# A normalised, gated FFN on one Trainium2 core: the second pair's down projection with tokens moving, and x turned through memory

## The chip, the cores and the metric

The kernel runs on one core of one Trainium2 chip. The metric is device time in microseconds of one execution. The kernel before has a median of 581.3 us over three runs (579.65 to 582.16). The profile is of one execution of the program.

The engines are named as in the profile: PE is TensorE (its weight loads are PEld), DVE is VectorE, ACT is ScalarE, POOL is GpSimd, SP is the queue of the sync engine, from which all transfers are issued here.

## The reference, cut to what matters

There are 2048 tokens of 512 channels. A layer normalisation, scaled and shifted by vectors from a condition, feeds a long convolution; its gated result is added to x. Then comes the part that this change touches:

```
h = layernorm(x) * (1 + cb) + sb          # per token, over 512 channels
g = silu(h @ w_gate)                      # 512 -> 1792
u = h @ w_up                              # 512 -> 1792
x = x + gb * ((g * u) @ w_down)           # 1792 -> 512
```

All of it is float32. The kernel splits each operand of these products into a high and a low part and multiplies in three passes (low x high, high x low, high x high).

## The kernel before

**Tokens and blocks.** x lies in four tiles `xt[0]` to `xt[3]`, of 128 tokens on the partitions by 4 rows of 512 channels each: four blocks of 512 tokens. Blocks 0 and 1 are the first pair, 2 and 3 the second.

**The FFN.** The 1792 hidden channels are cut into `NF` = 14 slices f of 128, two of which are a group g. The loop over n runs through the 14 slices for the first pair (q = 0, n = 2 to 13, the first two slices being done before it) and then again for the second (q = 1, n = 14 to 27). In this text a step is one n. A step makes gate and up for both blocks of the pair by seven products of half matrices instead of eight (Strassen-Winograd), each of six matmuls: two channel blocks by three passes, 128 x 128 stationary weights and 512 moving tokens. The products accumulate in PSUM tiles a, b, c (and d).

**Down.** Between the products stand groups of the down projection of slices that are finished. In the first pair and in the last group of the second, `down` uses 128 tokens of the activations as stationary operand and 512 output channels of w_down as moving one: six matmuls, and DVE adds the result to `xt` (`x<-x,dn`). In the other six groups of the second pair, `down_seven` applies the seven-product scheme over 2 slices, 2 blocks and 2 halves of 256 output channels: its stationary operand is 128 tokens of the activations, its moving one 256 columns of prepared weights (`wdb`, `wdt`). For each of two token pairs `i0` and each of seven products n it issues six matmuls, two token rows by three passes, into the two halves of one PSUM bank (da, db, dc), and DVE adds the bank to `xt[2 + t]`. Steps 16 to 27 each hold seven such groups, since a group's down follows two steps behind.

**The second norm of blocks 2 and 3.** While the first pair runs, the operands of the second are made. DVE takes mean and variance (`norm_stats`, steps 4 and 6), POOL turns them into scale and bias `rs`, and `norm2b` normalises two of the four rows of a block into a buffer `nn` of one copy, one row on ACT and one on DVE, twice per block. DVE turns 32 x 32 pieces in place (`half_t`). `half_put` writes the buffer to memory in four transfers; `half_get` reads it back in eight with channels on the partitions, into `hraw`. `half_s` applies the condition's scale and shift on ACT. Then `hraw` is split into the operands `B11`, `T1` and so on, from step 9 on.

**What sets the order.** Every engine works through its instructions in program order. The table `AT` and the calls of `also` hang functions on places (n, k): step n, behind the product numbered k. In a step the products run in the order 1, 5, 7, 2, 3, 6, 4 of these numbers (`PLACE`), so that (9, 7) is the third place of step 9 and (9, 4) its last. All transfers go through SP in program order: the weights of later steps (`ws`), the stores of prepared weights (`dw`, `ds`), w_down (`wds`), and the writes and reads of the norm. Weights are prepared on ACT, POOL and DVE a step ahead.

Of the kernel before, what the change touches and what calls it, by code (L numbers as in the profile page):

```python
# [27 lines left out]
G = 2  # L28
TB = 4
# [14 lines left out]
def adaln_h3_swiglu(ctx, tc, q, k0, v0, kT, vT, ssm, dskip, wgu, wdn, wmod, e_fwd, e_inv, w_c, out):  # L44
    nc = tc.nc
    pe, dve, act, pool, sp = (InOrder(tc, e) for e in (nc.tensor, nc.vector, nc.scalar, nc.gpsimd, nc.sync))
    cp = ctx.enter_context(tc.tile_pool(name="cp", bufs=1))
# [3 lines left out]
    dp = ctx.enter_context(tc.tile_pool(name="dp", bufs=1, space=bass.MemoryType.DRAM))  # L51
# [46 lines left out]
    ffn = {}  # L98
# [267 lines left out]
    away = {}  # L366
# [166 lines left out]
    def stats(xs, name, done=False, rows_=range(TB)):  # L533

        if name not in mvs:
            mvs[name] = cp.tile([P, 2 * TB], F32, name="mv" + name)
        mv = mvs[name]
        for i in rows_:
            if not done:
                bn[name, i] = cp.tile([P, 1, 6], F32, tag="bn1", name=f"bn{name}{i}", bufs=4)  # L540
                dve.bn_stats(bn[name, i][:, 0, :], xs[:, i, :])
            dve.bn_aggr(mv[:, 2 * i : 2 * i + 2], bn[name, i])
        if TB - 1 not in rows_:
            return None
        rs = cp.tile([P, 2, TB], F32, name="rs" + name)
# [7 lines left out]
    xt, st1 = {}, {}  # L553

    def load_x(t):
        a = e8([P, 4, D], F32, f"x{t}")
# [99 lines left out]

    raw_h, nrm = [], {}

    def norm2a(t, done=False):
        return stats(xt[t], f"b{t}", done)  # L660

    def norm2b(t, rs, h, split=True):

        n = nrm[t, h] = ffn["s"].tile([P, 2, D], F32, tag="nn", name=f"n{t}_{h}", bufs=1)
        for k in range(2):
            i = 2 * h + k
            if split and k:
                dve.tensor_scalar(
                    n[:, k], xt[t][:, i, :], rs[:, 0, i : i + 1], rs[:, 1, i : i + 1], op0=ALU.mult, op1=ALU.add
                )  # L670
            else:
                act.activation(
                    n[:, k], xt[t][:, i, :], AF.Identity, scale=rs[:, 0, i : i + 1], bias=rs[:, 1, i : i + 1]
                )

    NT = {}

    def norm_t(t, b):
# [15 lines left out]
        else:  # L694
            dve.tensor_scalar(dst, pt, sc, bi, op0=ALU.mult, op1=ALU.add)

    def half_t(t, h, k):

        v = nrm[t, h][:, k].rearrange("p (c x) -> p c x", x=32)
        dve.transpose(v, v)  # L700

    def half_put(t, h):

        v = nrm[t, h].rearrange("p k (c x) -> p (k c) x", x=32)
        m = away["n", t, h] = dp.tile([32, 32, 4, 32], F32, tag=f"n{t}{h}", name=f"naway{t}{h}")
        for z in range(4):
            sp.dma_start(m[:, :, z, :], v[32 * z : 32 * z + 32])

    def half_get(t, h):

        m = away["n", t, h].rearrange("d (k b y) z x -> y k d b (z x)", k=2, y=4)
        for y in range(4):
            for k in range(2):
# [47 lines left out]
    stage, AOP, WD, WG = {}, {}, {}, {}  # L761
# [114 lines left out]
    PASSES = ((1, 0), (0, 1), (0, 0))  # L876
# [14 lines left out]
    def down(q, g, t, i):  # L891

        parts = 2 if (q, g, t, i) == (1, NG - 1, 0, 3) else 1
        for h in range(parts):
            d = slice(h * D // parts, (h + 1) * D // parts)
            o = one("dn")[:, 0 : D // parts]
            for fl in range(G):
                for n, (wa, xa) in enumerate(PASSES):
                    pe.matmul(
                        o, acts[q, g * G + fl, t][:, xa, i * P : (i + 1) * P], WD[g][:, wa, fl, d],  # L900
                        start=(fl == n == 0), stop=(fl == G - 1 and n == 2),
                    )
            xv = xt[2 * q + t][:, i, d]
            dve.tensor_tensor(xv, xv, o, op=ALU.add)
            if g == NG - 1:
                sp.dma_start(out[:, 4 * (2 * q + t) + i, d], xv)
        if i == 3:
            for fl in range(G):
                slots.append(acts.pop((q, g * G + fl, t)))
# [7 lines left out]
    def down_seven(g, i0, n, bank_):  # L917

        k, t, dh = SUM[n]
        a, b = HOP[g][PROD[n][0]], WT[g][PROD[n][1]]  # L920
        more = k in bank_
        if not more:
            bank_[k] = one("d" + k)
        o = bank_[k].rearrange("p (i d) -> p i d", i=2)
        for ii in range(2):
            for m, (wa, xa) in enumerate(PASSES):
                pe.matmul(
                    o[:, ii], a[:, xa, (i0 + ii) * P : (i0 + ii + 1) * P], b[:, wa],
                    start=(not more and ii == m == 0), stop=(m == 2), skip_group_check=True,
                )  # L930
        xv = xt[2 + t][:, i0 : i0 + 2, dh * (D // 2) : (dh + 1) * (D // 2)]
        dve.tensor_tensor(xv, xv, o, op=ALU.add)
        if i0:
            slots.append(HOP[g].pop(PROD[n][0]))

    def sevens(g):
        for i0 in (0, 2):
            bank_ = {}
            todo.extend(("7", g, i0, n, bank_) for n in SUM)

    def downs(n):
        for _ in range(min(n, len(todo))):
# [681 lines left out]
    def release(n):  # L1624
# [32 lines left out]
    def also(n, k, fn, *a):  # L1657
        AT2.setdefault((n, k), []).append(lambda: fn(*a))

    for n, (t, h) in zip((6, 8, 10, 11), ((2, 0), (2, 1), (3, 0), (3, 1))):  # L1660
        also(n - 1, 2, half_t, t, h, 0)
        also(n - 1, 6, half_t, t, h, 1)
        also(n, 1, half_put, t, h)
        also(n, 3, half_get, t, h)
        also(n + 1, 5, half_s, t, h)
    for n in range(G, 2 * NF):
        q, f = n // NF, n % NF

# [110 lines left out]
```

## Time and profile before

| what | value |
|---|---|
| median of three runs | 581.3 us |
| span of the profiled execution | 577.7 us (the page gives no other time of it) |
| PE busy | 571.7 us, 99% |
| DVE, ACT, POOL busy | 448.3, 306.4, 318.0 us |
| granted TensorE clock | 1.000 |
| DMA | 106.98 MB, 185 GB/s |
| matmuls of 512 columns, a step of the first pair | 66 in 14.95 us |
| matmuls of 512 and 256 columns, a step of the second pair | 42 and 42 in 14.67 us |

Starts of instructions are counted from the start of the span. The steps that matter here start at 221.72 (step 5), 236.68, 251.63, 266.60, 281.56 (step 9), 296.80, 312.30 and 327.26 us (step 12); the down groups of the second pair run from 389.8 to 563.5 us. A row of the timeline gives start, length, engine, line and operation with output and inputs by the program's names; in brackets, how long the engine had been idle and what released it. Since one helper records every operation, all carry line 40; groups are told apart by their tiles.

### The profile page before, as it was taken

Reading aid. Unit: us, or ns where it says so; the run is one execution under the profiler, and the core shown is the slowest. Engines: PE = TensorE matmul, PEld = TensorE weight load, DVE = VectorE, ACT = ScalarE, POOL = GpSimd, SP = SyncE. Lnnn points to the kernel's source line nnn. Section 1 sums busy time; section 2 is a strip of 40 time slices with the busy share of each in tenths; the row PEclk is TensorE's granted clock in tenths of the full one; section 3 lists DMA queues with packets and bytes.
Section 4 is the critical chain, followed back from the end, with each engine's and each line's share of the span. In section 5 each row is a group of like instructions: output and inputs, shape, how many; then the busy total and the mean of one; then the engine's idle time right before and its main releaser. Section 6 shows DMA issues by size and latency. Waiting matters only on the chain.

```text
span 577.7 us, 10729 instructions
## 1 busy us (share of the span) xinstructions
PE 571.7 (99%) x4262; PEld 462.5 (80%) x4262; DVE 448.3 (78%) x622; ACT 306.4 (53%) x471; POOL 318.0 (55%) x298
## 2 busy tenths in 40 slices
PE   9999999999999999999999999999999999999997
PEld 9985476546888888888887888888888888888886
DVE  4999999998998766666576579858686868686766
ACT  3999989951754544445454566343424343434330
POOL 1349897689737866757475676461606161515210
PEclk9999999999999999999999999999999999999999
DMA  8966998998215454284939970454343434343403
GB/s 315 411 256 261 379 251 227 235 235 205 69 37 200 148 216 165 40 281 145 283 140 257 250 319 1 149 190 171 117 160 124 160 123 161 127 162 127 163 1 145
DMA packets 54435, 106.98 MB, mean 185 GB/s; under 512 B 19441, under 2 KB 36209, under 8 KB 48370
## 3 DMA queue, kind: packets, MB, share of 16 engines
q1 hardware_dynamic: 54386, 106.31, 56.0%
q8 instruction: 33, 0.54, 0.4%
q14 instruction: 16, 0.13, 0.1%
HBM read 71.69 MB, written 34.60 MB: 184 GB/s over the span
## 4 chain that ended last, share of the span: by engine, by line
PE 86%; DVE 5%; DMA 4%; ACT 1%; SPq 1%; issue 1%; POOL 0%; ACTq 0%; POOLq 0%; DVEq 0%
PE a L40 22%; PE dn L40 14%; PE c L40 11%; PE b L40 6%; PE da L40 6%; PE s L40 4%; PE g L40 4%; PE dc L40 3%; PE iv L40 3%; PE pk L40 3%; DMA wm<-in_wmod 2%; PE kvt L40 2%; PE px L40 2%; DMA away<-X 1%; PE kt L40 1%; PE db L40 1%
## 5 line engine op out<-in xcount | busy, mean ns | idle before, releaser
L40 PE MATMUL a<-op,wsum 128*128 128x512 f32 x432 | 110.9, 392 | 0.3 <-ACT r L40 0.2
L40 PEld LDWEIGHTS a<-op,wsum 128*128 128x128 f32 x432 | 78.7, 188 | 15.7 <-ACT r L40 0.7
L40 PE MATMUL dn<-wd,acts 128*128 128x512 f32 x360 | 90.4, 389 | 0.0
L40 PEld LDWEIGHTS dn<-wd,acts 128*128 128x128 f32 x360 | 67.5, 188 | 14.0
L40 ACT COPY p<-a 128x512 f32<-128x512 f32 x50 | 29.3, 587 | 57.2 <-PE a L40 57.2
L40 POOL TENSOR_TENSOR wa<-ws,wa 128x512 fp32r<-128x512 f32 (+1 forms) x28 | 32.9, 1196 | 41.1 <-ACT wa L40 41.1
L40 DVE TENSOR_TENSOR x<-x,dn 128x512 f32<-128x512 f32 (+1 forms) x65 | 43.4, 672 | 12.8 <-PE dn L40 12.5
L40 POOL TENSOR_TENSOR tb<-wds 128x256 f32<-128x256 f32 x12 | 8.9, 740 | 64.1 <-DVE wds L40 64.1
L40 DVE TENSOR_TENSOR b<-r,c 128x512 f32<-128x512 f32 x24 | 16.7, 696 | 32.9 <-ACT sg L40 32.9
L40 ACT COPY r<-a 128x512 f32<-128x512 f32 x24 | 14.1, 586 | 50.7 <-PE a L40 50.7
L40 PE MATMUL c<-op,wa 128*128 128x512 f32 x156 | 40.0, 392 | 0.0
L40 PE MATMUL c<-op,wsum 128*128 128x512 f32 x156 | 39.6, 389 | 0.0
L40 DVE STREAM_TRANSPOSE X<-X 128x1024 f32<-128x1024 f32 x16 | 37.6, 2415 | 0.8 <-ACT X L40 0.8
L40 POOL TENSOR_TENSOR wsum<-sr,wsum 128x512 fp32r<-128x512 f32 x28 | 38.1, 1381 | 0.0
L40 PE MATMUL b<-op,wa 128*128 128x512 f32 x144 | 36.9, 391 | 0.0
L40 POOL TENSOR_TENSOR wd<-wds,wd 128x512 fp32r<-128x512 f32 x14 | 18.3, 1329 | 29.1 <-ACT wd L40 29.1
L40 PEld LDWEIGHTS c<-op,wsum 128*128 128x128 f32 x156 | 29.3, 188 | 6.1
L40 DVE TENSOR_TENSOR x<-x,da 128x512 f32<-128x512 f32 x48 | 32.7, 681 | 1.2 <-PE da L40 1.1
L40 PEld LDWEIGHTS c<-op,wa 128*128 128x128 f32 x156 | 28.5, 188 | 5.7 <-DVE b L40 0.4
L40 PEld LDWEIGHTS b<-op,wa 128*128 128x128 f32 x144 | 26.3, 188 | 4.9
L40 POOL TENSOR_TENSOR s<-s,bcs 128x512 f32<-128x512 f32 x22 | 28.0, 1287 | 0.9
L40 POOL TENSOR_TENSOR sr<-ws 128x256 f32<-128x256 f32 x28 | 24.8, 885 | 5.3 <-issue 4.4
(193 smaller groups left out, 1351.1 us busy)
## 6 DMA issues: line engine op xcount, KB each, us to landing
ds<-wsum SPq DMA_DIRECT2D x12, 1024.0 KB, 8.0
wsum<-ds SPq DMA_DIRECT2D x12, 1024.0 KB, 6.4
dw<-wa SPq DMA_DIRECT2D x12, 768.0 KB, 6.3
wa<-dw SPq DMA_DIRECT2D x12, 768.0 KB, 4.3
ws<-in_wgu SPq DMA_DIRECT2D x16, 512.0 KB, 5.4
wds<-in_wdn SPq DMA_DIRECT2D x14, 512.0 KB, 7.1
wm<-in_wmod SPq DMA_DIRECT2D x6, 1024.0 KB, 10.1
away<-X SPq DMA_DIRECT2D x3, 2048.0 KB, 11.8
```

The costliest lines, as they stand in the source:

```text
L40: return lambda *a, **k: self.tc.keep_in_program_order(f(*a, **k))
```

## The change

Two things change together, because the first needs the second.

**Down with 512 tokens moving.** In `down_seven` the operands change sides: 128 of the 256 columns of the prepared weights are now stationary, and all 512 tokens of a block move. A group is three matmuls of 512 columns instead of six of 256. The same is done in `down` for the last group of the second pair, where both forms move 512 columns. The result has output channels on the partitions and tokens in the rows, so x of blocks 2 and 3 has to lie that way too, and the output is turned back after the kernel.

**x turned, and normalised after turning.** x itself is now turned: DVE turns 32 x 32 pieces of each row out of `xt` into the buffer (`turn`), `put_rows` writes it to memory in four transfers, and `get_rows` reads it back in four, twice as large as before, over `xt` itself. The statistics are turned as well (`turn_rs`), written in four tiny transfers (`put_rs`) and read back spread over all 128 partitions into `bcs` (`get_rs`). The norm is then a product and a sum with those rows, on two channel blocks at a time (`rows_op`, 128 x 1024, on DVE or POOL), and `rows_s` applies scale and shift on ACT with 512 columns instead of 256.

```diff
-    def norm2b(t, rs, h, split=True):
...
+    def turn(t, i):
+
+        h, k = i // 2, i % 2
+        if k == 0:
+            nrm[t, h] = ffn["s"].tile([P, NB * 4, 2, 32], F32, tag="nn", name=f"n{t}_{h}", bufs=1)
+        dve.transpose(nrm[t, h][:, :, k], xt[t][:, i].rearrange("p (c x) -> p c x", x=32))
+
+    def put_rows(t, h):
+
+        m = away["x", t, h] = dp.tile([32, NB * 4, 2, 4, 32], F32, tag=f"x{t}{h}", name=f"xaway{t}{h}")
         for z in range(4):
-            sp.dma_start(m[:, :, z, :], v[32 * z : 32 * z + 32])
...
+            sp.dma_start(m[:, :, :, z, :], nrm[t, h][32 * z : 32 * z + 32])
+
+    def get_rows(t, h):
+
+        m = away["x", t, h].rearrange("d (b y) k z x -> y d b (k z x)", y=4)
         for y in range(4):
-            for k in range(2):
-                i = (2 * h + k) * P
-                sp.dma_start(raw_h[0][32 * y : 32 * y + 32, t % 2, :, i : i + P], m[y, k])
...
+            sp.dma_start(xt[t][32 * y : 32 * y + 32, :, 2 * h * P : 2 * h * P + 2 * P], m[y])
+
+    def turn_rs(t):
+        dve.transpose(flat[t], flat[t])
+
+    def put_rs(t):
+
+        m = away["r", t] = dp.tile([2 * TB, 4, 32], F32, tag=f"r{t}", name=f"raway{t}")
+        for z in range(4):
+            sp.dma_start(m[:, z], flat[t][32 * z : 32 * z + 2 * TB])
+
+    def get_rs(t):
+        m = away["r", t].rearrange("(k i) z x -> k (i z x)", k=2)
+        sp.dma_start(bcs[:, 0:2, :], m.partition_broadcast(P))
+
+    def rows_op(t, a, k, e):
+
+        d = raw_h[0][:, t % 2, 2 * a : 2 * a + 2]
+        r = bcs[:, k, None, :].to_broadcast([P, 2, D])
+        e.tensor_tensor(d, d if k else xt[t][:, 2 * a : 2 * a + 2], r, op=ALU.add if k else ALU.mult)
+
+    def rows_s(t, a):
+
+        for b in (2 * a, 2 * a + 1):
+            d = raw_h[0][:, t % 2, b]
             act.activation(d, d, AF.Identity, scale=modT[:, 1, b : b + 1], bias=modT[:, 0, b : b + 1])
...
-        o = bank_[k].rearrange("p (i d) -> p i d", i=2)
-        for ii in range(2):
-            for m, (wa, xa) in enumerate(PASSES):
-                pe.matmul(
-                    o[:, ii], a[:, xa, (i0 + ii) * P : (i0 + ii + 1) * P], b[:, wa],
-                    start=(not more and ii == m == 0), stop=(m == 2), skip_group_check=True,
-                )
-        xv = xt[2 + t][:, i0 : i0 + 2, dh * (D // 2) : (dh + 1) * (D // 2)]
+        o = bank_[k]
+        for m, (wa, xa) in enumerate(PASSES):
+            pe.matmul(
+                o, b[:, wa, i * P : (i + 1) * P], a[:, xa],
+                start=(not more and m == 0), stop=(m == 2), skip_group_check=True,
+            )
+        xv = xt[2 + t][:, 2 * dh + i]
         dve.tensor_tensor(xv, xv, o, op=ALU.add)
...
+    plan(
+        2,
+        (5, 1, turn, 0),
+        (5, 5, turn, 1),
+        (5, 7, turn_rs),
+        (5, 3, put_rows, 0),
+        (5, 6, put_rs),
+        (6, 1, turn, 2),
+        (6, 7, turn, 3),
+        (6, 7, get_rs),
+        (6, 3, put_rows, 1),
+        (6, 4, get_rows, 0),
+        (7, 7, get_rows, 1),
+        (7, 6, rows_op, 0, 0, dve),
+        (7, 4, rows_op, 1, 0, pool),
+        (8, 6, rows_op, 0, 1, pool),
+        (8, 6, rows_s, 0),
+        (8, 4, rows_op, 1, 1, pool),
+        (9, 1, rows_s, 1),
+    )
...
```

Block 3 has a like plan: turns at (6, 4), (7, 4), (8, 3) and (8, 4), writes at (8, 1) and (9, 1), reads at (9, 6) and (10, 1), its products at (10, 2) on DVE and (10, 6) on POOL, its sums at (11, 1) on POOL and (11, 7) on DVE, scale and shift at (11, 3) and (12, 5).

How the plan lies in the engines' queues is seen at three places. The first is PE in step 16, where the second pair's down groups begin (a, b, c are the gate and up products, da, db, dc the down groups). Before:

```order
L40 MATMUL da<-wdb,acts 128x256 x6
L40 MATMUL a<-op,wsum 128x512 x6
L40 MATMUL dc<-wdt,acts 128x256 x6
L40 MATMUL b<-op,wa 128x512 x6
L40 MATMUL da<-wdt,acts_3931 128x256 x6
```

The same place of PE in the kernel after:

```order
L40 MATMUL da<-acts,wdb 128x512 x3
L40 MATMUL a<-op,wsum 128x512 x6
L40 MATMUL dc<-acts,wdt 128x512 x3
L40 MATMUL b<-op,wa 128x512 x6
L40 MATMUL da<-acts_3923,wdt 128x512 x3
```

The order is the same; each down group has three matmuls of twice the length.

The second place is ACT from the end of step 8 into step 9 (p1 and p2 are the copies of PSUM tile a behind the first and third product, n3_0 a row of block 3 that is normalised). Before:

```order
L40 CAST acts_1949<-a_3025 128x512
L40 COPY p1_3163<-a_3156 128x512
L40 CAST acts_1949<-c_3041 128x512
L40 ACTIVATE hraw_1934<-hraw_1934,modT_89 128x256 x4
L40 COPY p2_3192<-a_3156 128x512
L40 ACTIVATE n3_0_3194<-x3_790,rsb3_2882 128x512
L40 CAST wa_3197<-ws_3078 128x512
```

The same place of ACT in the kernel after:

```order
L40 CAST acts_1949<-a_3037 128x512
L40 ACTIVATE hraw_1934<-hraw_1934,modT_89 128x512 x2
L40 COPY p1_3179<-a_3172 128x512
L40 ACTIVATE hraw_1934<-hraw_1934,modT_89 128x512 x2
L40 CAST acts_1949<-c_3053 128x512
L40 COPY p2_3211<-a_3172 128x512
L40 CAST wa_3213<-ws_3090 128x512
```

The scale and shift of block 2 moved ahead of the copy p1 in one half and ahead of the cast in the other, and the normalising pass behind p2 is gone.

The third place is POOL in the same steps (wa, wsum and sr are gate and up weights being prepared). In the kernel after, behind the weights of step 9 and ahead of those of step 10:

```order
L40 TENSOR_TENSOR wa<-ws,wa 128x512
L40 TENSOR_TENSOR wa<-ws,wa 128x256
L40 TENSOR_TENSOR wsum<-sr,wsum 128x512 x2
L40 TENSOR_TENSOR hraw<-hraw,bcs 128x1024 x2
L40 TENSOR_TENSOR sr<-ws 128x256
L40 TENSOR_TENSOR sr<-sr,ws 128x256
```

The row of hraw is new: the two sums of block 2, for which the activations of the second place wait. Before, sr followed wsum directly.

More of the change, by code (lines that the diff above doesn't have):

```diff
@@ L544, in stats @@
             return None
-        rs = cp.tile([P, 2, TB], F32, name="rs" + name)
+        if name[0] == "b":
+            flat[int(name[1])] = f = cp.tile([P, 32], F32, name="rs" + name)
+            dve.memset(f, 0.0)
+            rs = f[:, 0 : 2 * TB].rearrange("p (k i) -> p k i", k=2)
+        else:
+            rs = cp.tile([P, 2, TB], F32, name="rs" + name)
         m, v = mv[:, 0::2], mv[:, 1::2]
@@ L551, in stats @@
         return rs
-    xt, st1 = {}, {}
+    xt, st1, flat = {}, {}, {}
     def load_x(t):
@@ L657, in adaln_h3_swiglu @@
     raw_h, nrm = [], {}
-    def norm2a(t, done=False):
-        return stats(xt[t], f"b{t}", done)
-    def norm2b(t, rs, h, split=True):
-        n = nrm[t, h] = ffn["s"].tile([P, 2, D], F32, tag="nn", name=f"n{t}_{h}", bufs=1)
-        for k in range(2):
[L666 to L669, printed above, removed]
-                )
[L671 to L674, printed above, removed]
     NT = {}
@@ L695, in norm_s @@
             dve.tensor_scalar(dst, pt, sc, bi, op0=ALU.mult, op1=ALU.add)
[L697 to L705, printed above, removed]
+    def turn(t, i):
[3 more added lines that the diff above has]
+        dve.transpose(nrm[t, h][:, :, k], xt[t][:, i].rearrange("p (c x) -> p c x", x=32))
@@ L898, in down @@
                 for n, (wa, xa) in enumerate(PASSES):
-                    pe.matmul(
-                        o, acts[q, g * G + fl, t][:, xa, i * P : (i + 1) * P], WD[g][:, wa, fl, d],
-                        start=(fl == n == 0), stop=(fl == G - 1 and n == 2),
-                    )
+                    w, x = WD[g][:, wa, fl], acts[q, g * G + fl, t][:, xa]
+                    l, r = (w[:, i * P : (i + 1) * P], x[:, d]) if q else (x[:, i * P : (i + 1) * P], w[:, d])
+                    pe.matmul(o, l, r, start=(fl == n == 0), stop=(fl == G - 1 and n == 2))
             xv = xt[2 * q + t][:, i, d]
@@ L905, in down @@
             if g == NG - 1:
-                sp.dma_start(out[:, 4 * (2 * q + t) + i, d], xv)
+                sp.dma_start(out[q, :, 4 * t + i, d], xv)
         if i == 3:
@@ L923, in down_seven @@
             bank_[k] = one("d" + k)
-        o = bank_[k].rearrange("p (i d) -> p i d", i=2)
-        for ii in range(2):
-            for m, (wa, xa) in enumerate(PASSES):
-                pe.matmul(
-                    o[:, ii], a[:, xa, (i0 + ii) * P : (i0 + ii + 1) * P], b[:, wa],
-                    start=(not more and ii == m == 0), stop=(m == 2), skip_group_check=True,
-                )
-        xv = xt[2 + t][:, i0 : i0 + 2, dh * (D // 2) : (dh + 1) * (D // 2)]
+        o = bank_[k]
[5 more added lines that the diff above has]
+        xv = xt[2 + t][:, 2 * dh + i]
         dve.tensor_tensor(xv, xv, o, op=ALU.add)
-        if i0:
+        if i:
             slots.append(HOP[g].pop(PROD[n][0]))
     def sevens(g):
-        for i0 in (0, 2):
+        for i in range(2):
             bank_ = {}
-            todo.extend(("7", g, i0, n, bank_) for n in SUM)
+            todo.extend(("7", g, i, n, bank_) for n in SUM)
     def downs(n):
@@ L1658, in also, with plan @@
         AT2.setdefault((n, k), []).append(lambda: fn(*a))
[L1660 to L1665, printed above, removed]
+    def plan(t, *steps):
+        for n, k, fn, *a in steps:
+            also(n, k, fn, t, *a)
+    plan(
[18 more added lines that the diff above has]
+    )
+    plan(
+        3,
+        (6, 4, turn, 0),
+        (7, 4, turn, 1),
+        (7, 4, turn_rs),
+        (8, 1, put_rows, 0),
+        (8, 2, put_rs),
+        (8, 3, turn, 2),
+        (8, 4, turn, 3),
+        (9, 1, put_rows, 1),
+        (9, 3, get_rs),
+        (9, 6, get_rows, 0),
+        (10, 1, get_rows, 1),
+        (10, 2, rows_op, 0, 0, dve),
+        (10, 6, rows_op, 1, 0, pool),
+        (11, 1, rows_op, 0, 1, pool),
+        (11, 7, rows_op, 1, 1, dve),
+        (11, 3, rows_s, 0),
+        (12, 5, rows_s, 1),
+    )
     for n in range(G, 2 * NF):
```

18 lines of the change are left out of this document (5 added, 13 removed).

## Prediction

> **What bounds the kernel now.** I read the page's busy row and clock first, then TensorE's (PE) waits, then busy time by step.
>
> ```profile
> span 577.7 us, 10729 instructions
> PE   571.7 (99%) x4262; PEld 462.5 (80%) x4262; DVE 448.3 (78%) x622; ACT 306.4 (53%) x471; POOL 318.0 (55%) x298
> PE a L40 <- ACT r L40: 0.2, 1, 0.2
> ```
>
> PE is busy 99% of the span, and this row is one of the few waits it has. But a busy PE need not be PE at its peak: a matmul's record (389 ns) is longer than the distance to the next one. So the distance between starts must be read. The windows below are one step each (columns: window, its length, busy time and count of PE, weight loads, DVE, ACT and POOL, granted clock, DMA share, GB/s): steps 6, 9 and 10 of the first pair, 18 and 19 of the second (from the first down group to the next step's).
>
> ```profile
> 236.68:251.63 14.95, 14.95 (x67) 12.38 (x66) 9.79 (x17) 6.46 (x12) 9.89 (x10) 1.00 0.64 183
> 281.56:296.80 15.24, 15.24 (x68) 12.31 (x66) 10.90 (x15) 9.18 (x16) 5.71 (x5) 1.00 0.71 242
> 296.80:312.30 15.50, 15.26 (x67) 12.31 (x66) 9.50 (x16) 7.52 (x13) 9.94 (x11) 1.00 0.66 180
> 419.49:434.15 14.66, 14.66 (x85) 12.89 (x84) 11.90 (x18) 5.04 (x9) 1.30 (x1) 1.00 0.44 164
> 434.15:448.83 14.68, 14.68 (x85) 12.90 (x84) 9.94 (x16) 6.17 (x11) 9.84 (x9) 1.00 0.34 127
> ```
>
> The clock is 1.00 throughout. A step of the first pair has 66 weight loads, so 66 matmuls of 512 columns, in 14.95 us: 0.2265 us each. A step of the second pair has 84: 42 of 512 columns (seven products) and 42 of 256 (seven down groups of six). If the 512 ones cost 42 x 0.2265 = 9.51 us there too, the 256 ones take 14.67 - 9.51 = 5.16 us, 0.1228 each: more than half of 0.2265. The starts say the same.
>
> ```profile
> 299.52 1.52 PE L40 MATMUL dn<-wd,acts 128*128 128x512 f32 x6
> 300.88 1.52 PE L40 MATMUL a<-op,wsum 128*128 128x512 f32 x6
> 403.45 1.52 PE L40 MATMUL c<-op,wsum 128*128 128x512 f32 x6
> 404.81 0.88 PE L40 MATMUL da<-wdb,acts 128*128 128x256 f32 x6
> 405.52 1.55 PE L40 MATMUL a<-op,wsum 128*128 128x512 f32 x6
> 406.91 0.88 PE L40 MATMUL dc<-wdt,acts 128*128 128x256 f32 x6
> ```
>
> Six matmuls of 512 take 1.36 us from start to start, whether the product changes (403.45 to 404.81) or a down group is followed by a product (299.52 to 300.88). Six of 256 take 0.71, and the 512 group behind them 1.39 instead of 1.36. So a 256 group costs 0.71 to 0.74 us where half a 512 group is 0.68.
>
> In both pairs, then, PE's issue sets the time, and small stalls hide inside its busy figure: steps 9 and 10 are longer than 14.95 by 0.29 and 0.55.
>
> **First part of the change: down with 512 tokens moving.** Each group of the second pair turns from six matmuls of 256 columns into three of 512. The same columns stream, with half the weight loads. There are twelve steps of seven groups:
>
> ```profile
> L40 PE MATMUL da<-wdb,acts x84: 277/283/283, 389.8 to 534.0; 128*128 128x256 f32 x84
> L40 PE MATMUL da<-wdb,op x60: 277/283/283, 401.3 to 563.4; 128*128 128x256 f32 x60
> ```
>
> These run from 389.8 to 563.5 us. A step afterwards is 63 x 0.2265 = 14.27 us, so it saves 14.67 - 14.27 = 0.40, and twelve of them **4.8 us**. The trace has groups of 512 among other 512 groups all through the first pair, so the price of the new form is taken from there; groups of three instead of six are not in the trace. Bounds: nothing, if the 0.71 and 1.39 belong to the changing between groups of different operands; and these 4.8. The last group pair keeps its 512-column matmuls, with operands swapped: nothing.
>
> Can VectorE (DVE) keep up with a step 0.4 us shorter? In even steps this is the tightest place:
>
> ```profile
> 421.59 0.88 PE L40 MATMUL dc<-wdt,op 128*128 128x256 f32 x6
> 422.50 0.69 DVE L40 TENSOR_TENSOR x<-x,dc 128x512 f32<-128x512 f32 x1 [0.51 <-PE dc L40]
> 425.65 0.68 DVE L40 TENSOR_TENSOR x<-x,da 128x512 f32<-128x512 f32 x1
> 426.50 0.76 PE L40 MATMUL da<-wdt,acts 128*128 128x256 f32 x5
> ```
>
> The da at 426.50 adds to a bank that the x<-x,da must have read. From dc's start to the end of that add is 4.74 us now, and 0.03 less with a shorter dc; PE needs 4.91 now, and 0.68 + 1.36 + 0.68 + 1.36 + 0.68 = 4.76 after. It just fits; I allow 0.05 in six steps, **0.3 us**.
>
> **Second part: x turned, norm with channels on partitions.** Removed in steps 5 to 12: four ScalarE (ACT) and four DVE passes that normalise a block's rows, and sixteen of the 32 reads back. Kept in number: eight DVE turns of 128x512 and sixteen writes. Added: two tiny turns, eight tiny writes and two reads of the statistics, and eight operations of 128x1024 (five on POOL, three on DVE). ACT's scale and shift come as eight of 512 columns for sixteen of 256. Only waits matter, since PE is not touched. The prices:
>
> ```profile
> L40 DVE TENSOR_TENSOR wds<-wds,bcs 128x1024 f32<-128x1024 f32 x13 | 16.7, 1281 | 0.0
> L40 DVE TENSOR_SCALAR n<-x,rsb 128x512 f32<-128x512 f32 x4 | 2.2, 543 | 2.4 <-DMA naway<-n 2.4
> L40 POOL TENSOR_TENSOR wds<-wds,bcs 128x1024 f32<-128x1024 f32 x1 | 2.4, 2380 | 0.0
> L40 POOL TENSOR_TENSOR v<-u,v 128x512 f32<-128x512 f32 x1 | 1.6, 1646 | 10.8 <-DVE u L40 10.8
> L40 ACT ACTIVATE n<-x,rsb 128x512 f32<-128x512 f32 x12 | 9.3, 811 | 6.7 <-POOL rsb L40 3.5 <-DMA naway<-n 3.2
> L40 ACT ACTIVATE hraw<-nt,modT 128x512 f32<-128x512 f32 x6 | 4.7, 775 | 2.6 <-PE nt L40 2.5
> ```
>
> DVE gains 3 x 1.28 and loses 4 x 0.54: 1.7 us over eight steps in which it idles about 5 of 15. POOL gains 5 x 2.38 = 11.9. The new wait with most behind it is ACT's scale and shift of block 2, which stands ahead of step 9's first copy out of PSUM and waits for POOL's second operation.
>
> ```profile
> 267.25 2.55 POOL L40 TENSOR_TENSOR wd<-wds,wd 128x512 fp32r<-128x512 f32 x2 [2.30 <-ACT wd L40]
> 275.43 2.53 POOL L40 TENSOR_TENSOR wsum<-sr,wsum 128x512 fp32r<-128x512 f32 x2
> 283.17 0.59 ACT L40 COPY p<-a 128x512 f32<-128x512 f32 x1 [0.83 <-PE a L40]
> 285.63 1.52 PE L40 MATMUL a<-op,wsum 128*128 128x512 f32 x6
> 285.87 2.08 ACT L40 ACTIVATE hraw<-hraw,modT 128x256 f32<-128x256 f32 x4 [0.85 <-DMA hraw<-naway]
> ```
>
> POOL is free at 269.8; the block's product (2.4) moves the end of its chain from 277.96 to 280.3 at most, and the first sum ends near 282.7. ACT then needs 1.5 us for the two activations and 0.6 for the copy: 284.8. PE adds to that bank at 285.63, so 0.8 us is to spare. With POOL at the dearest row (1.65 for 512, so 3.3 for 1024) product and sum end 1.8 later, and PE waits 1.0. The second sum holds ACT to about 286.6, where the old activations ended at 287.95. Behind them on ACT stand the cast that DVE's acts waits for and the second copy, no worse off than now.
>
> Steps 9 and 10 in turn lose what stalled them, passes that waited for a transfer to leave their buffer free:
>
> ```profile
> 300.77 2.97 SPq L40 DMA_DIRECT2D naway<-n  x4
> 306.33 0.82 ACT L40 ACTIVATE n<-x,rsb 128x512 f32<-128x512 f32 x1 [3.20 <-DMA naway<-n]
> 306.36 0.55 DVE L40 TENSOR_SCALAR n<-x,rsb 128x512 f32<-128x512 f32 x1 [2.39 <-DMA naway<-n]
> 309.45 1.66 PE L40 MATMUL a<-op,wsum 128*128 128x512 f32 x6 [0.24 <-ACT r L40]
> ```
>
> The write at 300.77 was through by 306.3, 5.5 us later. The new turns reuse that buffer as well; the nearest to its write is block 3's third, which I place 6.5 us behind it (step 8's last DVE work to its fifth place). I take back **0.8 us** (0.29 + 0.55), bounds 0 and 0.8.
>
> The transfers stay on SP's queue (rows of the writes, and of the reads back from issue to landing):
>
> ```profile
> naway<-n SPq DMA_DIRECT2D x16, 128.0 KB, 3.2
> L40 SPq DMA_DIRECT2D hraw<-naway x32: 303/720/1294, 245.9 to 329.3; - x32
> DMA to landing us min/median/max: 2.2/5.2/8.1
> 283.70 0.69 DVE L40 TENSOR_TENSOR c<-sg,c 128x512 f32<-128x512 f32 x1
> 303.60 1.52 PE L40 MATMUL b<-op,wa 128*128 128x512 f32 x6
> ```
>
> Block 3 is the later one. Its last turn follows the DVE row at 283.70, so about 285.1. Four writes, three weight transfers, the statistics and eight reads at 0.72 us each are issued by about 296 and land 5.2 later, near 301. DVE wants the rows behind product b of step 10 (start 303.60), at about 306: 5 us to spare. Behind SP's wait stand weight transfers that are used a step later. Block 2 has more room. For small new waits that I cannot name I take **0.3 us**, bounds 0 and 3.6 (each of steps 8 to 12 as bad as the mean of steps 9 and 10 now, 5 x 0.42, plus the 1.0 at step 9, plus another 0.5 at step 10).
>
> **Sum.** 577.7 - 4.8 - 0.8 + 0.3 + 0.3 = 572.7 us of span. The page gives no time beyond its span; the median of the runs is 581.3, 3.6 above it. I carry these 3.6 over: 576.3.
>
> **Rivals.** *(A) The moving length is worth nothing.* If columns alone cost, or the 0.03 to 0.06 us per group belong to changing between groups of different matmuls, only the 0.8 minus 0.6 of the other terms is left: 581.1. For it: the difference per matmul is a few per cent and the ends are modelled. Against: first-pair groups change stationary tile and PSUM bank just as often, at 1.36. By the Trainium skill, "TensorE: Matmul & The Clock Gate", section Back-to-back issue gap, a matmul takes N/2.4 + 2.5 ns: 109.2 and 215.8 ns, 2.5 ns saved per pair, by its estimate 0.6 us in all and a time near 580.5. The trace's 226.5 and 122.8 ns don't agree with it. Chance 0.10.
>
> *(B) New waits eat the gain.* ACT behind POOL in steps 8 and 9, DVE in step 10: 576.3 - 0.3 + 3.6 = 579.6. For: in-order engines, and POOL's 12 us more. Against: the slacks above. Chance 0.13.
>
> *(C) The turned rows come late, slower.* DVE's first product of block 3 waits for its reads. At the worst rows (1.29 us an issue; 8.1 to landing for reads) they land near 309, a 3 us wait, and waits of 2.4 and 3.2 cost PE 0.55 in step 10, so some 2.6 us are absorbed. Slower by over 0.5% (584.2) needs 7.9 us more than the forecast, so a wait of 10.5, reads landing at 316, three times the slowest. For: the DMA share is 0.71 in step 9, and a read spread over 128 partitions is not in the trace. Against: half the reads, each twice as large. It would cost 584 to 586. Chance 0.06.
>
> **Numbers.** My forecast has 0.71, its own range 574.8 to 578.3. About 0.5% (2.9 us) is what a measurement of this kernel tells from no change. Faster (under 578.4) takes the forecast and a fifth of B: 0.74. Slower is C and a little of B: 0.07. The rest, 0.19, is the same. The range goes from 574.4 (no new waits at all, 575.7, and a fast median: three runs of before differ by 2.5) to 580.2, into B and most of the way to A.
>
> **What would show it.** Matmuls of 512 columns for da, db and dc; steps of 14.27 us in the second pair; step 10 at 14.95; ACT's scale and shift ending before 284.2 in step 9. A second-pair step above 14.5 us would make the first term wrong; a first-pair step above 15.5 the second.

## The result, and the profile after

The changed kernel takes **575.98 us** (median of six runs, 574.91 to 576.35) against 581.45 us for the kernel before in runs beside them (579.26 to 582.33): a ratio of 0.9912, 95% interval 0.9892 to 0.9933. In a second comparison it was 575.79 against 581.66, 0.9898 (0.9871 to 0.9926). The prediction was 576.3.

The page of the changed kernel, its busy row, and the row of PE's waits that is new:

```profile
span 574.1 us, 10193 instructions
PE 568.3 (99%) x4010; PEld 449.5 (78%) x4010; DVE 452.8 (79%) x625; ACT 302.0 (53%) x459; POOL 329.1 (57%) x303
PE da L40 <- DVE x L40: 0.2, 1, 0.2
```

The same 99% as before, with 252 matmuls fewer (84 groups of three instead of six). The execution took 575.92 us in all, so 1.8 us lie around its span. Its steps 9, 10, 16, 18 and 19 (columns as in the prediction):

```profile
282.32:297.28 14.96, 14.96 (x68) 12.39 (x66) 10.55 (x14) 9.82 (x15) 11.68 (x10) 1.00 0.92 269
297.28:312.24 14.96, 14.96 (x68) 12.39 (x66) 9.91 (x13) 6.41 (x12) 13.47 (x12) 1.00 1.02 333
387.04:401.86 14.82, 14.57 (x64) 11.75 (x63) 11.49 (x19) 5.46 (x10) 4.73 (x4) 1.00 0.43 162
416.14:430.56 14.42, 14.42 (x64) 11.75 (x63) 11.88 (x19) 5.31 (x10) 3.44 (x4) 1.00 0.45 165
430.56:444.84 14.28, 14.28 (x64) 11.82 (x63) 9.95 (x15) 5.88 (x11) 7.68 (x7) 1.00 0.33 129
```

Steps 9 and 10 are 14.96, where they were 15.24 and 15.50. In the second pair the odd step 19 is 14.28, the forecast; the even step 18 is 14.42, and step 16, the first with down groups, 14.82 (it was 14.96 before, where the others were 14.67). Steps 20, 22, 24 and 26 are like 18, and step 27 took about 14.43. Against 14.28 that is 0.54 + 6 x 0.14, about 1.4 us. Before, only step 16 had such a loss, 0.29.

So in place of 12 x 0.40 = 4.8 us the second pair gave 176.4 - 172.75 = 3.6 (before 14.96 + 11 x 14.675, after 12 x 14.28 + 1.4). Where the 0.14 is lost shows in the timeline of step 18:

```profile
420.90 0.84 PE L40 MATMUL dc<-op,wdt 128*128 128x512 f32 x3
423.74 0.69 DVE L40 TENSOR_TENSOR acts<-c,acts 128x512 fp32r<-128x512 f32 x1 [0.66 <-ACT acts L40]
424.34 0.69 DVE L40 TENSOR_TENSOR b<-p,b 128x512 f32<-128x512 f32 x1
424.76 0.64 PEld L40 LDWEIGHTS db<-acts,wdb 128*128 128x128 f32 x3
424.94 0.68 DVE L40 TENSOR_TENSOR x<-x,da 128x512 f32<-128x512 f32 x1
424.98 0.84 PE L40 MATMUL db<-acts,wdb 128*128 128x512 f32 x3
425.67 0.53 PEld L40 LDWEIGHTS da<-acts,wdt 128*128 128x128 f32 x3 [0.27 <-DVE x L40]
425.67 0.96 PE L40 MATMUL da<-acts,wdt 128*128 128x512 f32 x3
426.47 1.31 PE L40 MATMUL a<-op,wsum 128*128 128x512 f32 x5
```

From dc's start to the end of the x<-x,da at 424.94 are 4.72 us (the prediction had 4.71). PE had the matmul's turn at 425.66, 4.76 after dc, as predicted, and the matmul did start at 425.67. But its weight load would have started 0.22 us earlier, as that of db does (424.76 against 424.98). The wait holds the weight load too, and so the group takes 0.80 us to the next start instead of 0.68.

### The profile page after: what moved, and what is told of

The parts are those of the page before. It is cut to its first block, busy times and chain, and to the rows that moved or that the text cites. A ratio compares the mean times of both kernels' runs of the same rounds, so it can differ in the third digit from the quotient of the medians.

```text
span 574.1 us, 10193 instructions
## 1 busy us (share of the span) xinstructions
PE 568.3 (99%) x4010; PEld 449.5 (78%) x4010; DVE 452.8 (79%) x625; ACT 302.0 (53%) x459; POOL 329.1 (57%) x303
## 4 chain that ended last, share of the span: by engine, by line
PE 95%; ACT 3%; DVE 2%; issue 0%; POOL 0%; ACTq 0%; POOLq 0%; DVEq 0%
PE a L40 23%; PE dn L40 15%; PE c L40 12%; PE b L40 6%; PE da L40 6%; PE s L40 4%; PE iv L40 4%; PE g L40 4%; PE pk L40 4%; PE kt L40 3%; PE dc L40 3%; PE px L40 3%; PE kvt L40 2%; PE y L40 2%; PE db L40 1%; PE warm L40 1%
## 5 line engine op out<-in xcount | busy, mean ns | idle before, releaser
L40 PEld LDWEIGHTS a<-op,wsum 128*128 128x128 f32 x432 | 81.0, 188 | 17.4 <-ACT p L40 0.4
L40 PE MATMUL dn<-wd,acts 128*128 128x512 f32 x336 | 84.8, 389 | 0.0
L40 PEld LDWEIGHTS dn<-wd,acts 128*128 128x128 f32 x336 | 63.1, 188 | 13.1
L40 POOL TENSOR_TENSOR wsum<-sr,wsum 128x512 fp32r<-128x512 f32 x28 | 40.0, 1452 | 0.0
L40 POOL TENSOR_TENSOR xs<-xs 128x512 f32<-128x512 f32 x14 | 19.1, 1393 | 15.4 <-ACT xs L40 15.4
```

Of the source, the lines that this page charges most:

```text
L40: return lambda *a, **k: self.tc.keep_in_program_order(f(*a, **k))
```

## Experiments

The theory: each 512-column group saves about 0.06 us over its 256-column form, DVE's order costs 0.14 of it in every even step, and the rest of the gain is two stalls of steps 9 and 10. The main rival was A, that the moving length is worth nothing and the turn made the gain.

Step 2 started between 180.7 and 184.0 us in the profiles of these runs, though all but one (256 columns in the first pair) have the same work ahead of it, so single profiles are best compared from there. The table gives, for each, the start of step 2, the span less that start, and the length of the steps in question.

| kernel | step 2 at | from there to the end | step 9 | step 10 | steps 16 / 18 / 19 |
|---|---|---|---|---|---|
| before, the prediction's profile | 181.95 | 395.7 | 15.24 | 15.50 | 14.96 / 14.67 / 14.68 |
| before, once more | 183.30 | 397.3 | 16.61 | 15.60 | 14.95 / 14.68 / 14.68 |
| change | 182.72 | 391.4 | 14.96 | 14.96 | 14.82 / 14.42 / 14.28 |
| change, once more | 182.89 | 391.5 | 14.95 | 14.96 | 14.85 / 14.44 / 14.28 |
| down alone | 181.92 | 393.1 | 16.01 | 15.61 | 14.83 / 14.42 / 14.28 |
| turn alone | 182.31 | 395.1 | 14.96 | 14.96 | 14.95 / 14.68 / 14.68 |

### The kernel before, once more

> The kernel before, profiled once more. The sum of the prediction was made against one profile with a span of 577.7 us and took 3.6 us around the span; the changed kernel shows 1.8 us around its span. Theory: what lies around the span is 1.8 here too, and the profile before was of a quick execution; then this span is 577.5 to 580.5, 1.8 below its own time, and what differs from the first profile lies before step 2's start (181.95 us there). Rival: it lies in steps 9 and 10, whose passes wait for a write to memory (15.24 and 15.50 us there, more here). Steps of the second pair 14.67, first of them 14.96.

It took 582.42 us with a span of 580.6: 1.8 us around the span here too. Both causes hold a part. Step 2 starts 1.35 us later than in the first profile, and steps 9 and 10 are 1.37 and 0.10 longer. So the profile on which the sum was built was of a quick execution, and the stalls of steps 9 and 10 are not 0.84 us but 2.3 in this one. Its rows from step 9 (the last is the last group of that step):

```profile
288.73 2.08 ACT L40 ACTIVATE hraw<-hraw,modT 128x256 f32<-128x256 f32 x4 [2.20 <-DMA hraw<-naway]
293.66 1.05 ACT L40 CAST spare<-hraw 128x1024 fp32r<-128x1024 f32 x1
294.75 2.17 DVE L40 TENSOR_TENSOR spare<-hraw,spare 128x1024 fp32r<-128x1024 f32 x1 [2.01 <-ACT spare L40]
298.18 1.66 PE L40 MATMUL c<-op,wa 128*128 128x512 f32 x6 [1.27 <-DVE b L40]
```

ACT waits 2.20 us for block 2's rows to come back from memory; in the first profile it was 0.85. Part of the difference arises in SP's queue: the last of the eight reads was issued at 286.65, 3.6 us after the start of step 9, where it was 1.7 us in the first profile (283.24). Ahead of it SP waits for an older store of other data, `ds<-wsum`, to land, 3.2 us here and 1.1 there by the profiles' lists of waits. That store is not all of it: in the run with the down alone, the next one, SP waited 1.3 us for it and ACT 1.60. Two experiments further down follow the chain behind ACT.

### Down alone

```diff
-        o = bank_[k].rearrange("p (i d) -> p i d", i=2)
...
-                    o[:, ii], a[:, xa, (i0 + ii) * P : (i0 + ii + 1) * P], b[:, wa],
+                o, b[:, wa, i * P : (i + 1) * P], a[:, xa],
...
-        xv = xt[2 + t][:, i0 : i0 + 2, dh * (D // 2) : (dh + 1) * (D // 2)]
+        xv = xt[2 + t][:, 2 * dh + i]
```

> Only the down projection with 512 tokens moving; the norm and its transfers as before (the down sums go to x as if it were turned, which it is not: the turning of x is left out). Theory (the gain comes from the 512 columns): steps of the second pair as in the changed kernel, 14.28 and 14.42 us in turn, first 14.82; steps 9 and 10 stalled as before, by 0.3 and 0.55; so 0.8 us above the changed kernel, 576.8, 4.7 under before. Rival A (moving length is worth nothing, the turn made the gain): second-pair steps 14.67, 580.9 or more.

576.64 us (median of ten), 0.9930 of before (0.9910 to 0.9950). Steps 9 and 18:

```profile
281.65:297.66 16.01, 15.25 (x67) 12.31 (x66) 10.91 (x15) 9.17 (x16) 5.80 (x5) 1.00 0.72 233
...
417.18:431.60 14.42, 14.42 (x64) 11.75 (x63) 11.88 (x19) 5.31 (x10) 3.43 (x4) 1.00 0.46 165
```

The second pair is that of the changed kernel, even to the 0.14 of the even steps: rival A falls. The stalls of steps 9 and 10 stay, here 1.05 and 0.65. From step 2 on it is 1.7 us above the changed kernel, all of it these two steps.

### The turn alone

Shown against the kernel before:

```diff
-        (5, 7): lambda: norm2b(2, rs[2], 0),
...
+        (5, 1, turn, 0),
+        (5, 5, turn, 1),
...
+        (6, 4, get_rows, 0),
```

> Only the turning of x and the norm with channels on partitions; the down projection with 256 columns moving as before (it adds to rows that are now turned: the matching form of down is left out). Theory: steps 5 to 15 all 14.96 us, stalls of 9 and 10 gone, second-pair steps 14.67; 0.8 us under before, 580.6. Rival A: nearly all the gain is here, 576.5. If the kernel before waits longer in steps 9 and 10 in most executions than in its one profile, between the two, 578.5 to 580.

578.63 us (median of ten), 0.9965 of before (0.9939 to 0.9991): 2.8 us, more than the 0.8 of the sum and less than rival A's 5. Steps 9 and 10 are 14.96 and step 18 is 14.68 (9 and 18 here):

```profile
281.94:296.90 14.96, 14.96 (x67) 12.39 (x66) 10.56 (x14) 9.82 (x15) 11.69 (x10) 1.00 0.91 264
...
416.29:430.97 14.68, 14.68 (x87) 12.90 (x85) 11.93 (x19) 5.13 (x10) 3.26 (x3) 1.00 0.43 162
```

From step 2 on it is 0.6 under the first profile of before and 2.2 under the second, and 3.7 above the changed kernel. The steps of the two parts add up to the change. The medians of the two parts (4.8 and 2.8 us) add up to 2.1 more than the change's 5.5; with step 2 starting anywhere within 3 us, ten runs don't settle such a difference, and the steps do.

### The first pair's down with 256 columns

```diff
+            for c in range(1 if q else 2):
...
+                        e = slice(c * H, (c + 1) * H)
+                        oc, l, r = ... (o[:, e], x[:, i * P : (i + 1) * P], w[:, e])
```

> The changed kernel with the first pair's 56 down groups as twelve matmuls of 256 columns in place of six of 512, into the same bank: the price of the disputed form by itself. Theory: two times 0.057 us more for a group (84 groups of six gave 4.8 us), 56 x 0.114 = 6.4 us: 582.4, first-pair steps of four such groups 15.4. Rival A (moving length is worth nothing): 576.0, steps of 14.96.

581.31 us (median of ten), 5.3 above the changed kernel where 6.4 were expected. Step 6 and two groups with what follows them:

```profile
239.85:255.21 15.36, 15.36 (x91) 13.63 (x90) 10.41 (x18) 6.37 (x12) 9.88 (x10) 1.00 0.96 272
242.57 1.60 PE L40 MATMUL dn<-wd,acts 128*128 128x256 f32 x12
244.00 1.55 PE L40 MATMUL a<-op,wsum 128*128 128x512 f32 x6
245.39 1.60 PE L40 MATMUL dn<-wd,acts 128*128 128x256 f32 x12
```

With the same operands, bank and columns, each group costs 0.40 / 4 = 0.10 us more. 0.07 is inside the group (1.43 from start to start where six of 512 take 1.36) and 0.03 in the 512-column group behind it (1.39). The price of the short form is real, and it has two parts: some 6 ns a matmul, and 0.03 us a change from 256 columns back to 512. Rival A's zero would have left the step at 14.96.

### The change, once more

> The changed kernel once more, beside the others of this call. Second-pair steps 14.28 and 14.42 us in turn, the first 14.82; steps 5 to 15 all 14.96; 575 to 576.5 in all. If its median among runs of one chip lies nearer 575 than 576, the 1 us between the single parts' medians and their steps (the down alone stood 0.7 above the changed kernel where its steps say 1.7) was the front of the runs compared.

575.79 us (median of six, 574.47 to 576.33), and the steps as forecast, the even ones at 14.44. The median stands hardly nearer 575, so the difference between the medians of the single parts and their steps is not cleared up by it.

### DVE's order in the even steps

```diff
-                operand(g, "S4", x)
+                h = HOP.setdefault(g, {})["S4"] = slots.pop(0)
+                act.copy(h[:, 0], x)
+                low.append(lambda: dve.tensor_tensor(h[:, 1], x, h[:, 0].bitcast(F32), op=ALU.subtract))
...
         dve.tensor_tensor(b, p1, b, op=ALU.add)
+        while low:
+            low.pop(0)()
...
+        if (q, f) == (1, NF - 1):
+            finish(1)
         behind(1)
```

> The changed kernel, and on VectorE in the second pair's even steps the subtraction that ends the operand S4 stands behind b<-p,b instead of ahead of it; in the last step the cast and subtraction of the step before stand ahead of the last wds product. Theory (PE waits at da for an x<-x,da that is queued on VectorE behind an operation that waits for ScalarE): the 0.14 us of every even step and of the last step and the 0.54 of the first go; all twelve steps 14.28, 1.3 us under the changed kernel. Rival (the 0.14 is the price of two groups on one bank with a product between, whatever VectorE does, or x<-x,da is late anyway): even steps stay at 14.42, no gain.

574.76 us (median of six) beside 575.79 for the changed kernel; against before 0.9875 (0.9842 to 0.9908). Steps 16 and 18, and rows of step 18:

```profile
388.33:402.64 14.31, 14.31 (x64) 11.82 (x63) 11.49 (x19) 5.46 (x10) 4.73 (x4) 1.00 0.44 168
416.92:431.20 14.28, 14.28 (x64) 11.82 (x63) 11.89 (x19) 5.30 (x10) 3.43 (x4) 1.00 0.45 166
423.92 0.70 DVE L40 TENSOR_TENSOR b<-p,b 128x512 f32<-128x512 f32 x1
424.53 0.68 DVE L40 TENSOR_TENSOR acts<-c,acts 128x512 fp32r<-128x512 f32 x1
425.13 0.68 DVE L40 TENSOR_TENSOR x<-x,da 128x512 f32<-128x512 f32 x1
426.22 0.64 PEld L40 LDWEIGHTS da<-acts,wdt 128*128 128x128 f32 x3
```

DVE does b<-p,b in the time that it spent waiting for ACT's cast; x<-x,da ends at 425.81 and the weight load starts on its time. Steps 17 to 27 are all 14.28, step 16 is 14.31. From step 2 on it takes 390.0 us, about 1.4 under the changed kernel, where 1.3 was expected. The intervals of the two medians overlap, so the gain of 1.0 in the medians is not shown by the times alone; the steps show it. By its median it is the quickest of the versions tried.

### One more pass on POOL ahead of step 9

```diff
+        (8, 6, rows_op, 1, 0, pool),
         (8, 6, rows_op, 0, 1, pool),
         (8, 6, rows_s, 0),
```

> The changed kernel with one more pass of 128x1024 on POOL (block 2's product of the second half, done twice, 2.40 us) ahead of block 2's first sum: the price of rival B's wait. Theory (the copy out of PSUM of step 9 stands behind the scale and shift, which wait for POOL, and had 1.0 us to spare: ended 285.33, wanted 286.40): step 9 longer by 1.4 us, 16.4 in place of 14.96, the copy behind a wait for POOL; steps 8 and 10 at 14.96. If the waits behind it (the acts cast, the second copy) take more, up to 17.3. Rival (ScalarE's queue is no path to PE): 14.96 throughout.

Step 9 took 16.43 us, steps 8 and 10 14.96 and 14.97. In the changed kernel and then in this one:

```profile
283.34 1.52 ACT L40 ACTIVATE hraw<-hraw,modT 128x512 f32<-128x512 f32 x2 [0.24 <-POOL hraw L40]
284.77 0.56 ACT L40 COPY p<-a 128x512 f32<-128x512 f32 x1
286.40 1.52 PE L40 MATMUL a<-op,wsum 128*128 128x512 f32 x6
```

```profile
286.46 1.52 ACT L40 ACTIVATE hraw<-hraw,modT 128x512 f32<-128x512 f32 x2 [2.59 <-POOL hraw L40]
287.89 0.56 ACT L40 COPY p<-a 128x512 f32<-128x512 f32 x1
288.50 1.65 PE L40 MATMUL a<-op,wsum 128*128 128x512 f32 x6 [1.18 <-ACT p L40]
```

Of the 2.40 us, 1.47 reached PE. So the wait of rival B exists at the place where the prediction put it, and had 0.93 us to spare (it was put at 0.8). The waits behind it took nothing more.

### DVE's product apart from POOL's

```diff
-        (7, 6, rows_op, 0, 0, dve),
+        (8, 5, rows_op, 0, 0, dve),
```

> The changed kernel with VectorE's product of block 2 moved from step 7's sixth product to step 8's fifth, so that it no longer starts with POOL's product (270.10 and 270.21 us; POOL's took 3.38 us there, 2.40 for block 3). Theory (two such passes on sbuf wait for each other): POOL's product takes 2.40; VectorE's 1.2, or up to 0.7 more if it meets one of POOL's weight sums of 0.74, which is then longer instead. Rival (POOL's product was slow for its reads of x): 3.38 again. No step's length changes, 14.96.

No step changed. First POOL's and DVE's rows in the changed kernel, then in this one:

```profile
270.10 1.23 DVE L40 TENSOR_TENSOR hraw<-x,bcs 128x1024 f32<-128x1024 f32 x1
270.21 3.38 POOL L40 TENSOR_TENSOR hraw<-x,bcs 128x1024 f32<-128x1024 f32 x1
306.12 3.52 POOL L40 TENSOR_TENSOR wsum<-sr,wsum 128x512 fp32r<-128x512 f32 x2
306.24 2.24 DVE L40 TENSOR_TENSOR hraw<-x,bcs 128x1024 f32<-128x1024 f32 x1
```

```profile
269.29 2.42 POOL L40 TENSOR_TENSOR hraw<-x,bcs 128x1024 f32<-128x1024 f32 x1
272.48 1.60 POOL L40 TENSOR_TENSOR sr<-sr,ws 128x256 f32<-128x256 f32 x1
271.89 1.59 DVE L40 TENSOR_TENSOR hraw<-x,bcs 128x1024 f32<-128x1024 f32 x1
```

Apart from DVE's product, POOL's takes 2.42 us. The product now meets POOL's sr passes: it is 0.36 longer, and one sr pass takes 1.60 instead of 0.74. In the changed kernel whichever began first ran at its own length (DVE at 270.10), and the other was longer by about what was left of it (POOL 3.38 for 2.40; at 306.24 DVE 2.24 for 1.23, while POOL's two passes took 3.52 for 2.54). The Trainium skill, "SBUF — State Buffer", section SBUF: two separate sides, has it that VectorE, where it reads two inputs from SBUF, and GpSimd take one pair of ports in turn, the later one waiting for the whole instruction of the other. The rows agree with that.

### Step 9 of the kernel before: what is it long by?

```diff
-        (10, 7): lambda: norm2b(3, rs[3], 1),
+        (10, 3): lambda: norm2b(3, rs[3], 1),
...
-        also(n - 1, 2, half_t, t, h, 0)
+        also(n - 1, 6 if n == 11 else 2, half_t, t, h, 0)
...
-        also(n + 1, 5, half_s, t, h)
+        also(n + 1, 7 if n == 8 else 5, half_s, t, h)
```

> The kernel before with its two waits of steps 9 and 10 moved under cover and nothing else: block 2's second scale and shift one product later in step 9 (the seventh product in place of the fifth), block 3's second normalising pass two products later in step 10, its two turns behind it. Theory: step 9 is long by what ScalarE waits for the reads back of block 2 less 0.55 us (waits of 0.85, 1.60 and 2.20 us gave 0.29, 1.05 and 1.65), and step 10 by the pass that waits 3.2 us for the write to leave its buffer (0.55 to 0.65); both steps 14.96 now, second-pair steps 14.67, and the median 1.6 to 2.3 us under the kernel before, 579.2 to 579.9, as the turn alone (578.6) had it. Rival (both steps are long by the write and its buffer, as the prediction put it): step 10 at 14.96, step 9 still 15.2 to 16.6; the median 0.6 under.

581.94 us (median of twelve), 0.9996 of before (0.9981 to 1.0011). Half of the expectation failed. Step 10 is 14.96: that stall was the pass that waited for the write to leave its buffer. Step 9 is 16.64:

```profile
289.61 2.08 ACT L40 ACTIVATE hraw<-hraw,modT 128x256 f32<-128x256 f32 x4
295.14 2.18 DVE L40 TENSOR_TENSOR spare<-hraw,spare 128x1024 fp32r<-128x1024 f32 x1 [2.00 <-ACT spare L40]
298.58 1.65 PE L40 MATMUL c<-op,wa 128*128 128x512 f32 x6 [1.29 <-DVE b L40]
```

ACT no longer waits for the reads, but the scale and shift, moved one place, begin as late as they did with the wait. What follows from them on ACT (the casts of the next weights, then that of B11 into `spare`) is as late too, and DVE's subtraction of 2.18 us waits 2.00 for that cast. Behind it stands b<-r,c, and for that PE waits. The rival's number for step 9 came true, but nothing in step 9 waits for a write. The subtraction itself is long, too: `op<-hraw,op`, as large and also from SBUF, takes 1.22 us on DVE at 340.46 in the first profile of before, and POOL's two sums beside the subtraction took 3.51 us here instead of 2.54, so the two passes met as in the experiment before this one. What step 9 would lose without that meeting was not tried. DVE's idle time ahead of that subtraction was 0.66, 1.43, 2.01 and 2.00 us in the four profiles of this form, and the step long by 0.28, 1.05, 1.65 and 1.68: 0.32 to 0.38 less each time.

The next run therefore left the scale and shift where they were, kept the later pass in step 10, and took the cast and subtraction of B11 out of step 9:

```diff
-        (9, 2): lambda: ahead("B11", "B11"),
+        (10, 2): lambda: ahead("B11", "B11"),
```

> The kernel before with block 3's second normalising pass two products later (as in the run before it) and, in place of the later scale and shift, the cast and subtraction of the second pair's operand B11 moved from step 9 to step 10; ScalarE's wait for block 2's reads stays where it was. Theory (step 9 is long by a chain: reads back, ScalarE's scale and shift, its cast of B11, VectorE's subtraction of 2.16 us, then b<-r,c, for which PE waits; VectorE's idle time ahead of the subtraction less 0.37 us is the stall: 0.66, 1.43, 2.01 and 2.00 gave 0.28, 1.05, 1.65 and 1.68): with the cast and the subtraction out of step 9 it is 14.96 even where ScalarE waits 1 to 2 us for the reads; step 10 at 14.96 to 15.2; the median 1.5 to 2.3 us under the kernel before, 579.3 to 580.1. Rival (PE waits in step 9 for a copy behind the late scale and shift, not for VectorE): step 9 still 15.2 to 16.6, the median 0.6 under at most.

579.22 us (median of twelve) beside 580.85, 0.9971 (0.9954 to 0.9988). Steps 9 and 10, and ACT's row in step 9:

```profile
281.93:296.89 14.96, 14.96 (x67) 12.39 (x66) 9.43 (x13) 7.88 (x14) 5.09 (x5) 1.00 0.76 250
296.89:312.29 15.40, 15.27 (x67) 12.31 (x66) 12.02 (x17) 8.81 (x14) 13.02 (x13) 1.00 0.62 162
287.63 2.08 ACT L40 ACTIVATE hraw<-hraw,modT 128x256 f32<-128x256 f32 x4 [2.23 <-DMA hraw<-naway]
```

ACT waits 2.23 us for the reads and the step is 14.96 all the same: in step 9 the reads delay PE only by way of DVE's subtraction. Step 10 now loses 0.44, in a down group at its start: its fifth weight load, at 300.82, waits 0.54 us for DVE's `acts<-a,acts`. Why that one is late was not tried.

### Block 3's reads made twice

```diff
         (10, 1, get_rows, 1),
+        (10, 1, get_rows, 0),
+        (10, 1, get_rows, 1),
```

> The changed kernel with block 3's eight reads of turned rows made twice, the second time over the first: rival C's lateness, by some 9 us of issue (eight took 9.2 us). Theory (VectorE's first product of block 3 at 306.24 found its rows landed no more than 2.6 us earlier, since the last read was issued at 300.9 and reads take at least 2.7 to land; PE then bears some 2.6 us of VectorE's wait): VectorE waits 6.5 to 9 us, and step 10 is 4 to 6.5 us longer, 19 to 21.5. Rival (the slack is the 5 us of the prediction): VectorE waits 4 us, step 10 is 1.5 us longer, 16.5. If the reads' weight transfers behind them come late too, step 11 is longer as well.

Step 10 took 16.55 us, step 11 14.96. SP's reads in the changed kernel, then SP's and DVE's rows in this one:

```profile
292.29 9.18 SPq L40 DMA_DIRECT2D x<-xaway  x8
```

```profile
290.30 14.06 SPq L40 DMA_DIRECT2D x<-xaway  x16
307.86 1.22 DVE L40 TENSOR_TENSOR hraw<-x,bcs 128x1024 f32<-128x1024 f32 x1 [3.52 <-DMA x<-xaway]
```

Eight more reads took only 4.9 us more to issue, not 9, so neither expectation had its delay right, and that the rival's 1.5 us came out is no sign for it. The 9.18 us of the changed kernel are not all issue: ahead of its last two reads SP waits for older transfers to land, 0.6 us for the store `ds<-wsum` and 1.8 us for `bcs<-raway`, the read of the statistics over 128 partitions. DVE waits 3.52 of the 4.88. If the rows land as much later as they are issued later, they had landed 1.4 us before DVE wanted them in the changed kernel; PE, which lost 1.59, bears 1.9 us of DVE's wait.

## Why the prediction was right, point by point

That the time came so near (575.98 for 576.3) is in part luck. Two terms were missed by about the same amount in opposite directions: DVE's catching up cost 0.8 to 1.1 us more than the 0.3 allowed, and the stalls of steps 9 and 10 gave back 0.9 to 1.5 us more than the 0.8 counted.

**The first term, 4.8 us for 512 columns, was right in size.** Odd steps are 14.28, and with DVE's order mended all but step 16 (14.31) are: 12 x (14.67 - 14.28) = 4.7. The estimate of 0.6 us by the rule of the Trainium skill ("TensorE: Matmul & The Clock Gate", section Back-to-back issue gap), which that section calls the gap of an isolated matmul, is not what the runs show. The prediction's reading, that a 256 group costs 0.03 to 0.06 more than its columns, holds for other operands too (0.10 for twelve matmuls in the first pair). The fear that a part belongs to changing between groups was half true: 0.03 of some 0.06 is such a change. It goes with the 256 columns all the same.

**DVE's catching up, 0.3 us, was mis-sized: it costs 1.4 us** (1.1 more than what step 16 lost before). The step that failed is "PE needs 4.91 now, and ... 4.76 after. It just fits; I allow 0.05 in six steps". Both times were right to 0.01 us. But the end of DVE's add was set against the start of the matmul, while the wait holds its weight load, 0.22 us ahead: the add had 4.54 us and took 4.72. That gives the 0.14 of six steps. The 0.54 of step 16 was not seen: there DVE's subtraction that waits for ACT comes later still, and the weight load at 396.96 waited 0.67 us. Step 16, at 14.82, is thereby above the 14.5 that the prediction named as a sign against its first term; since it falls to 14.31 with DVE's order mended, it speaks against this second one:

```profile
396.96 0.53 PEld L40 LDWEIGHTS da<-acts,wdt 128*128 128x128 f32 x3 [0.67 <-DVE x L40]
```

**The stalls of steps 9 and 10, 0.8 us, were fully taken back, but are larger in other executions**: 0.84 in the profile of the prediction, 2.3 and 1.7 in the two others with that norm and its order. The turn alone gave 2.8 us in the median. The prediction put both stalls down to a write that leaves its buffer late. That holds for step 10. Step 9's chain is another: reads back, ACT's scale and shift, its cast of B11, DVE's subtraction, b<-r,c. Its length follows the landing of transfers, so one profile can't price it. In the prediction, the row with ACT's wait of 0.85 us for the reads was quoted, for ACT's time alone.

**The 3.6 us around the span was 1.8.** The other 1.8 lay in the profile, which was of a quick execution: short stalls, and an early step 2. The short stalls belonged into the gain; the spread ahead of step 2 is in both kernels and doesn't. In the medians, then: 3.6 from the second pair and 1.7 to 2.3 from steps 9 and 10, 5.3 to 5.9 us, where 5.5 and 5.9 were measured.

**New waits, 0.3 us, were nothing.** The one at ACT behind POOL was named rightly, with 0.8 us to spare for 0.93 measured. ACT's first scale and shift ended at 284.86, 2.54 after the step's start; the bound of 284.2 was 2.64 after it.

**The rivals.** A fell by three runs (down alone, turn alone, 256 columns in the first pair). B's wait exists and cost nothing; from 0.93 us of delay on it would have. C's slack was overrated: the prediction had the rows landed 5 us early, and by the run with the reads made twice it was 1.4. It took 0.72 us an issue; the eight reads of block 3 took 9.18 us, 0.55 to 1.32 for an issue and 2.4 of SP's waits for older transfers, and the last was issued at 300.9 instead of 296. The longest of these waits was for the read over 128 partitions, which the prediction had named as not in its trace. PE bears 1.9 of DVE's wait instead of 2.6. For 0.5% slower the reads would have had to be about 1.4 + 1.9 + 7.9 = 11 us later still.

## What to carry to other kernels

Where a matmul waits for a PSUM bank, set the release against the start of its first weight load, not against that of the matmul: here 0.22 us decided whether a chain that "just fits" does. A stall that hangs on the landing of a transfer can't be priced from one profile; look for it in several executions, and count it as the part of the gain that varies. On an in-order engine, an operation that waits for another engine's answer should stand behind work that is ready: moving one subtraction behind one ready pass, with a like move in the last step, gave back 1.4 us.

## What the runs showed of the hardware that was not expected

- Short groups pay in two places: some 6 ns more a matmul for the same columns (1.43 us for twelve of 256, 1.36 for six of 512), and 0.03 us once, in the group of 512 columns that follows (1.39 for 1.36). Every matmul here has its own weight load; which of the two costs the 6 ns was not tried. Groups of only three matmuls of 512 cost no more than those of six (step of 63 in 14.28 us, 0.2267 each).
- A wait that delays a matmul's start by 0.01 us costs 0.12 to 0.14, since its weight load is not under the matmul ahead.
- Two passes on SBUF tiles, one on DVE and one on POOL, don't run at the same time: the later is longer by nearly the rest of the other (3.38 us for 2.40, 2.24 for 1.23). DVE's passes with one input from PSUM do: beside five of them of 0.65 to 0.70, POOL's two sums of block 2 took 4.76 together from 280.91 on, 2.38 each.
- SP holds a read back until an older transfer of other data has landed: the last read of block 2 for `ds<-wsum`, 1.1 us in the first profile of before and 3.2 in the second, and the last read of block 3 for `bcs<-raway`, 1.8 us in the changed kernel. Why it waits was not tried.
- The part of the program ahead of step 2, which the change doesn't touch, ends anywhere from 180.7 to 184.0 us in the twelve profiles that have it as it was. What in it varies was not tried.
